# Attention and mixture of experts on one core: V in quadrants, a new order inside the turn, a cap on routing's steps

## Chip, core and metric

One core of a Trainium2 chip runs the whole program. The metric is the device time of one execution in microseconds. The kernel before takes 719.83 us in the median of three runs.

## What is computed

First a local and global attention (4 batches, 8 heads, 768 tokens, head size 64; a token sees itself, the 95 tokens before it and the first 8), then a mixture of 8 experts with two experts a token.

```python
scores = scale * np.matmul(q, k.transpose(0, 1, 3, 2)) + bias
scores = np.where(is_global | is_local, scores, -1e9)
a = np.exp(scores - np.max(scores, -1, keepdims=True))
x = np.matmul(a / (a.sum(-1, keepdims=True) + 1e-9), v)      # then (3072, 512)
noisy = x @ w_gate + np.log1p(np.exp(x @ w_noise)) * noise
top2 = ...                                                    # the two largest of 8, softmax over them
for e in range(8):
    out[mask] += top2_w * (np.maximum(x[mask] @ w1[e], 0.0) @ w2[e])
```

## The kernel before

The order of the work is written out by hand; nothing reorders it, and each engine takes its instructions in that order.

**The attention stage** is a loop of 48 turns, one for each unit: four heads of one block of 128 tokens (24 blocks, 6 a batch). A turn `n` handles several units at different depths: `score(n + 2)` (VectorE adds the bias and takes the maximum out of PSUM, ScalarE takes the exponential), `trans(n)` and `trans(n + 1)` (PE transposes the weights, ScalarE copies them), `gate_t` in every second turn (the tokens of a finished block are transposed on PE, copied by ScalarE, and copied in halves by GpSimd for a store), `product(n + 4)` (PE multiplies q and k), `attend(n - 2)` (PE multiplies the weights with V; each head has 65 columns, the last of ones, which gives the sum), `norm(n - 4)` (VectorE divides by that sum), and in every fourth turn `gate_l`, the products with the gate's weights, which read what ScalarE copied for `gate_t`.

The 128 tokens of a block are two halves of 64 (`s`), the four heads are two (`x`) by two (`y`). Each half sees a window of 168 keys: 96 before, 8 global, 64 own. `attend` sums the halves of a head in two rounds of matmuls; a matmul's place in the PE array is `tile_position`, and the first round of a block that has a block before it uses 64 rows of the array, the second up to 128:

```python
parts = [[(vs[g], 0, Q, 2), (vp[g], 0, NP + NG, 0)], [(vp[g], Q, NP + NG, 2), (vs[g], 0, P, 1)]]
```

`vs` holds the V rows of the block, `vp` the 96 rows before it and the 8 global ones. The sums of one unit lie in one PSUM bank; units alternate between banks 5 and 6. Scores lie in banks 0 and 1, transposed weights in 3 and 4.

**Routing** is a generator, `route(r)`, for each of 5 segments of blocks. It yields after each small VectorE instruction, and the loop takes one step of it at a `tick(place)` between the instructions of `score` (places 0 to 3) and `norm` (4 to 6), and up to 3 or 5 in `finish()` at the turn's end. A step that waits for another engine is marked, and is due again at a later place of the next turn. Segment `CLOSE` (number 2) closes expert 0's first 512 tokens: its masks are made on GpSimd (`mask`), summed on PE, and then expert 0's four tiles of tokens are gathered by GpSimd (`gather`, one a turn), copied (`whole_words`) and turned on PE (`turn`). After the loop what is left of that segment is run out, and the experts' products (`up`, `down`) begin.

In eight turns of the stage a split of w1 into a high and a low part runs as well (`split`: ScalarE and GpSimd).

## Time and profile before

| what | us or share |
|---|---|
| median of 3 runs (719.52 to 723.66) | 719.83 |
| the profiled execution's own time | 718.65 |
| its span | 716.9 |
| PE, VectorE, ScalarE, GpSimd busy | 97%, 64%, 61%, 45% |

An execution's time is its span and about 1.75 us around it. PE is TensorE's matmuls, PEld its weight loads, DVE is VectorE, ACT ScalarE, POOL GpSimd. A float32 matmul leaves two records. Times inside the trace count from the span's start. In the chain of waits a line is one piece of the path that ended last; a bracket in the timeline gives the idle time of the engine ahead of the instruction and who ended it.

### The profile page before, as it was taken

How to read it: one execution, taken by the hardware profiler on the slowest of the kernel's cores; microseconds unless marked ns; L12 is line 12 of the kernel's file. 1: busy time of each engine (PE TensorE's matmuls, PEld its weight loads, DVE VectorE, ACT ScalarE, POOL GpSimd, SP SyncE). 2: the span in 40 equal slices, each digit the busy share in tenths (PEclk: the TensorE clock that was granted, in tenths of full speed). 3: DMA queues.
4: the chain of work that ended last, by engine and by line, in shares of the span. 5: the costliest groups of instructions: out<-in, count | busy, mean ns of one | idle time of the engine just before them, and what ended most of it. 6: DMA issues, size and time to landing. Idle time of an engine off the chain costs nothing.

```text
span 716.9 us, 16231 instructions
## 1 busy us (share of the span) xinstructions
PE 692.7 (97%) x5769; PEld 618.3 (86%) x5769; DVE 457.1 (64%) x1473; ACT 440.0 (61%) x922; POOL 323.3 (45%) x416
## 2 busy tenths in 40 slices
PE   7999999999999799999999999999999999999995
PEld 5888888787789699999799989999899898889984
DVE  7669888977946376746564665576376756656600
ACT  6888787662437496546664685587467646755511
POOL 3363626481087362164606462644555344632222
PEclk9999999999999999999999999999999999999999
DMA  8996778685098784167916792587459547843233
GB/s 252 336 279 216 216 233 289 203 299 188 0 261 181 155 141 118 27 120 160 207 16 133 158 217 48 118 174 165 75 148 201 108 121 166 185 74 89 31 45 47
DMA packets 129913, 111.10 MB, mean 155 GB/s; under 512 B 51578, under 2 KB 96762, under 8 KB 129824
## 3 DMA queue, kind: packets, MB, share of 16 engines
q1 hardware_dynamic: 118416, 83.84, 42.9%
q0 software_dynamic: 11264, 25.89, 20.1%
q8 instruction: 47, 0.77, 0.5%
q14 instruction: 42, 0.34, 0.2%
q10 hardware_dynamic: 144, 0.26, 0.1%
HBM read 71.07 MB, written 27.59 MB: 138 GB/s over the span
## 4 chain that ended last, share of the span: by engine, by line
PE 64%; DVE 10%; issue 8%; DMA 7%; POOL 5%; ACT 5%; POOLq 0%; SPq 0%; ACTq 0%; DVEq 0%
PE bank L1397 20%; PE av L1144 19%; PE av L1167 7%; PE av L874 4%; PE sc L823 4%; PE at L853 3%; DMA xt<-xg 3%; DMA xg<-xd,ids 2%; DVE wall L196 2%; PE at L1107 1%; ACT hh L1088 1%; DVE w2l L196 1%; POOL out_dram L1120 1%; DVE ns L837 1%; DMA xd<-xt 1%
## 5 line engine op out<-in xcount | busy, mean ns | idle before, releaser
L1397 PE MATMUL bank<-xh,wall 128*128 128x384 f32 (+4 forms) x784 | 216.3, 343 | 1.1 <-ACT aside L1438 0.9
L1397 PEld LDWEIGHTS bank<-xh,wall 128*128 128x128 f32 x784 | 143.5, 188 | 6.7 <-DVE wall L196 1.4
L1397 PE MATMUL bank<-xl,wall 128*128 128x384 f32 (+4 forms) x392 | 133.4, 340 | 0.0
L1144 PE MATMUL av<-w2h,hh 128*128 128x512 f32 x304 | 120.3, 396 | 4.0 <-ACT aside L1176 2.3
L1120 POOL DMA_INDIRECT out_dram<-y,ids x40 | 63.8, 1596 | 127.7 <-ACT y L1117 124.4
L1144 PE MATMUL av<-w2h,hl 128*128 128x512 f32 x304 | 119.5, 393 | 0.3 <-DVE hl L1092 0.3
L1144 PE MATMUL av<-w2l,hh 128*128 128x512 f32 x304 | 119.1, 392 | 0.0
L196 DVE TENSOR_TENSOR wall<-raw,wall 128x512 fp32r<-128x512 f32 (+1 forms) x84 | 73.0, 875 | 48.4 <-ACT wall L195 48.3
L1092 DVE SCALAR_TENSOR_TENSOR hl<-bank,hh 128x384 fp32r<-128x384 f32 (+4 forms) x84 | 47.1, 561 | 66.5 <-ACT hh L1088 66.3
L195 ACT ACTIVATE wall<-raw 128x512 fp32r<-128x512 f32 (+1 forms) x84 | 58.0, 698 | 43.2 <-POOL raw L1252 43.2
L243 POOL DMA_INDIRECT xg<-xd,ids x53 | 58.8, 1109 | 52.1 <-DVE place L293 32.5
L840 ACT ACTIVATE a<-ns,mx 128x168 f32<-128x168 f32 (+1 forms) x192 | 67.9, 422 | 19.3 <-DVE mx L837 18.6
L1397 PEld LDWEIGHTS bank<-xl,wall 128*128 128x128 f32 x392 | 73.9, 188 | 2.7
L275 ACT ACTIVATE xg<-xt 128x1024 uint16<-128x1024 uint16 (+3 forms) x46 | 60.0, 1307 | 19.7 <-DMA xt<-xg 19.6
L1144 PEld LDWEIGHTS av<-w2h,hl 128*128 128x128 f32 x304 | 57.1, 188 | 14.1 <-DVE hl L1092 1.5
L1144 PEld LDWEIGHTS av<-w2h,hh 128*128 128x128 f32 x304 | 57.1, 188 | 14.0 <-ACT aside L1176 2.5
L1144 PEld LDWEIGHTS av<-w2l,hh 128*128 128x128 f32 x304 | 57.1, 188 | 9.3 <-DVE w2l L196 0.3
L837 DVE CUSTOM_DVE_ANT_0 ns<-sc,bias 128x168 f32<-128x168 f32 (+1 forms) x188 | 51.7, 319 | 18.4 <-PE sc L823 12.3
L1251 POOL TENSOR_TENSOR raw<-raw 128x256 f32<-128x256 f32 x28 | 21.9, 781 | 85.8 <-DVE wall L196 85.4
L874 PE MATMUL av<-vs,at 128*64 128x65 f32 (+1 forms) x768 | 57.3, 224 | 0.0
L235 POOL COPY xt<-y 128x256 uint16<-128x256 uint16 x96 | 35.2, 405 | 49.0 <-DVE y L890 46.9
L1088 ACT ACTIVATE hh<-bank 128x384 fp32r<-128x384 f32 (+4 forms) x84 | 41.8, 497 | 23.6 <-DVE bank L1467 16.0
(214 smaller groups left out, 1485.6 us busy)
## 6 DMA issues: line engine op xcount, KB each, us to landing
raw<-in_w SPq DMA_DIRECT2D x64, 256.0 KB
raw<-in_w SPq DMA_DIRECT2D x32, 512.0 KB
out_dram<-zero SPq DMA_DIRECT2D x14, 512.0 KB
vs<-in_v SPq DMA_DIRECT2D x24, 260.0 KB
xd<-xt SPq DMA_DIRECT2D x24, 256.0 KB
qbuf<-in_q SPq DMA_DIRECT2D x23, 256.0 KB
ks<-in_k SPq DMA_DIRECT2D x20, 272.0 KB
vp<-in_v SPq DMA_DIRECT2D x20, 195.0 KB
```

Of the source, the lines that this page charges most:

```text
L195: nc.scalar.activation(hi, src, AF.Copy)
L196: eng.tensor_sub(lo, src, hi.bitcast(F32))
L243: nc.gpsimd.indirect_dma_start(out=xg[e, t].bitcast(U16)[:m], out_offset=None, in_=xd[:n], in_offset=bass.IndirectOffsetOnAxis(ap=r, axis= ...
L275: nc.scalar.activation(words(x), xt.pop((e, t)).rearrange("p (h k) t -> p h (k t)", h=2), AF.Copy)
L837: nc.vector.tensor_tensor_reduce(out=ns[x][:, s, :w], in0=ps[:, s], in1=bias[:, u + x, s] if i else bias0[:, u + x, s], scale=-scale, scal ...
L840: nc.scalar.activation(A[n + x][:, s * w:(s + 1) * w], ns[x][:, s, :w], AF.Exp, bias=mx[x][:, s:s + 1], scale=-1.0)
L874: nc.tensor.matmul(ps[s * Q:(s + 1) * Q, h], a[r:z, part * P + q0:part * P + q0 + Q], t[r:z, c], start=k == 0 and (n == 1 or h == 0), stop ...
L1088: nc.scalar.activation(inner(e)[0][j][:, f, :src.shape[1]], src, AF.Relu)
L1120: ins = nc.gpsimd.indirect_dma_start(out=out, out_offset=bass.IndirectOffsetOnAxis(ap=r, axis=0), in_=y, in_offset=None, bounds_check=N + ...
L1144: nc.tensor.matmul(ps, x[j][:, f, cols], w[:, f], start=n == 0, stop=n == 3 * FC - 1)
L1167: nc.tensor.matmul(to, w[:, f, cols], x[:, f], start=n == 0, stop=n == 3 * FC - 1)
L1397: nc.tensor.matmul(ps, wb[c % 2][u][:, 2 * a + k], x[v][:, 2 * b + k], start=start and n == 0, stop=stop and n == 5, skip_group_check=True)
```

## The change

`attend` gives every head's two halves as eight matmuls of up to 128 rows and then eight of 64 x 64, which are placed in the four quadrants of the array. For that the second head of a pair (`x` = 1) has its halves and its V rows in another order: the exponentials are written to other columns, which are shifted by 24, the host lays V out anew in two tiles of 128 rows for each block (`vp` now has 128 rows, one transfer, instead of 96 and 8 in two), and the two heads of a pair sum into two banks. All units use both banks, in three places by turns. `norm` comes first in the turn, `attend` comes ahead of `product`, and the ticks have new places. Each of the first three segments may take 7, 8 or 9 steps a turn.

```diff
+        if b in AV and "av" in pools:
+            return pools["av"][:, AV.index(b)]
...
-                nc.sync.dma_start(vp[g][:NP], v[b, i - 1, P - NP:])
-                if i <= 4:
-                    nc.sync.dma_start(vp[g][NP:], v[b, 0, :NG])
+                nc.sync.dma_start(vp[g], v[b, i, 1])
...
+        PACE = {0: 7, 1: 8, 2: 9}
+        left = {}
...
         def begin():
+            left.update(PACE)
             for x, _ in active:
                 x.ready = {WAIT: 4, WAIT + 1: 6}.get(x.ready, 0)
...
             for y in sorted(active, key=lambda y: y[1] != CLOSE):
-                if y[0].ready <= place:
+                if y[0].ready <= place and left.get(y[1], 1) > 0:
                     return go(y)
...
-                    nc.scalar.activation(A[n + x][:, s * w:(s + 1) * w], ns[x][:, s, :w], AF.Exp,
+                    a = (1 - s) * w + Q - GQ if x and i else s * w
+                    nc.scalar.activation(A[n + x][:, a:a + w], ns[x][:, s, :w], AF.Exp,
                                          bias=mx[x][:, s:s + 1], scale=-1.0)
-                    tick(2 * x + s)
+                    tick(3 + 2 * x + s)
...
-            ps = pav[g, u // 2] = bank("av")[:, :4 * D1].rearrange("p (h d) -> p h d", h=4)
+            c0 = n // 2 % 3 * 2 * D1
+            ps = pav[g, u // 2] = av[:, :, c0:c0 + 2 * D1].rearrange("p x (y d) -> p x y d", y=2)
+            rounds = [[(s, x, vs, s, 0, P) for x in range(2) for s in range(2)]]
             if i:
+                rounds = [
+                    [(0, 0, vp, 0, 0, NP + NG), (1, 0, vs, 1, 0, P), (0, 1, vs, 1, 0, P), (1, 1, vs, 2, 0, P)],
+                    [(0, 0, vs, 2, 0, Q), (0, 1, vp, 0, Q, Q), (1, 0, vp, 2, Q, GQ), (1, 1, vp, 0, 0, Q)],
+                ]
+            for k, parts in enumerate(rounds):
+                for y in range(2):
+                    for s, x, t, part, r, m in parts:
+                        c = ((x * 2 + u // 2) * 2 + y) * D1
+                        nc.tensor.matmul(ps[s * Q:(s + 1) * Q, x, y], at[x][r:r + m, part * P + y * Q:][:, :Q],
+                                         t[g][r:r + m, c:c + D1], start=k == 0 and y == 0,
+                                         stop=k + 1 == len(rounds),
                                          tile_position=(r, s * Q), skip_group_check=True)
...
                 begin()
+                if n >= 4:
+                    norm(n - 4)
                 if n + 2 < NPAIR:
                     score(n + 2)
                 trans(n)
...
+                if n >= 2:
+                    attend(n - 2)
                 if n + 4 < NPAIR:
                     product(n + 4)
                 if n == NPAIR - 2:
-                    attend(n - 2)
-                if n >= 4:
-                    norm(n - 4)
-                if n == NPAIR - 2:
                     gate_t(NT - 2)
-                elif n >= 2:
-                    attend(n - 2)
```

On PE, turn 26 of the loop (a unit without a block before it) stands before as follows; `at` are the transposed weights, `m` is the bank of tokens and gate, `sc` the scores, `av` the products with V:

```order
L853 MATMUL at<-ident,a_185 128x128 x3
L853 MATMUL at<-ident,a_186 128x128 x3
L371 MATMUL m<-ident,y_98 128x128 x4
L823 MATMUL sc<-ks,qbuf_113 64x168 x8
L874 MATMUL av<-vs,at 64x65 x8
L393 MATMUL m<-pair,wgn 32x128 x8
```

The same turn after:

```order
L872 MATMUL at<-ident,a_188 128x128 x3
L872 MATMUL at<-ident,a_189 128x128 x3
L378 MATMUL m<-ident,y_98 128x128 x4
L894 MATMUL av<-vs,at 64x65 x8
L837 MATMUL sc<-ks,qbuf_117 64x168 x8
L400 MATMUL m<-pair,wgn 32x128 x8
```

V and the scores have changed places; what reads the tokens' copy (`m<-pair`) is still the last of the turn.

On GpSimd, at the end of the stage, before: `wall` are the closing segment's masks, `xt<-y` a block's copies of tokens, `xg<-xd` the gathers of expert 0, `xg<-xg` the copies of what was gathered.

```order
L555 TENSOR_SCALAR wall<-iota_p,aside 128x128 x10
L235 COPY xt<-y_98 128x2x128 x4
L243 DMA xg<-xd,ids_87 128x1024
L235 COPY xt<-y_97 128x2x128 x4
L243 DMA xg<-xd,ids_87 128x1024 x2
L235 COPY xt<-y_98 128x2x128 x4
L243 DMA xg<-xd,ids_87 128x1024
L235 COPY xg<-xg 128x2x128 x4
L235 COPY xt<-y_97 128x2x128 x4
L235 COPY xg<-xg 128x2x128 x12
```

The same place after:

```order
L562 TENSOR_SCALAR wall<-iota_p,aside 128x128 x10
L242 COPY xt<-y_98 128x2x128 x4
L242 COPY xt<-y_97 128x2x128 x4
L250 DMA xg<-xd,ids_87 128x1024 x3
L242 COPY xt<-y_98 128x2x128 x4
L242 COPY xt<-y_97 128x2x128 x4
L250 DMA xg<-xd,ids_87 128x1024
L242 COPY xg<-xg 128x2x128 x16
```

The gathers stand a turn later, and the fourth stands behind the last copies of tokens, with all sixteen copies behind it.

## Rows read from the trace of the kernel before

**Rows 1.** The page: span, and busy time of each engine

```profile
span 716.9 us, 16231 instructions
PE 692.7 (97%) x5769; PEld 618.3 (86%) x5769; DVE 457.1 (64%) x1473; ACT 440.0 (61%) x922; POOL 323.3 (45%) x416
```

**Rows 2.** Busy time by stretch: length, engines, granted clock, DMA share, GB/s

```profile
30.20:41.95 11.75, 11.75 (x249) 10.35 (x245) 7.02 (x46) 10.37 (x30) 5.20 (x7) 1.00 1.06 335
53.74:71.08 17.34, 16.75 (x333) 14.44 (x329) 15.80 (x109) 14.25 (x40) 6.35 (x15) 1.00 0.71 223
137.51:146.35 8.84, 8.04 (x126) 6.62 (x122) 7.43 (x44) 5.41 (x15) 8.53 (x15) 1.00 0.11 36
```

**Rows 3.** Chain of waits, 69 to 77 us: start, length, engine, tile, line

```profile
69.34 0.73 PE sc L823 x16
...
71.15 0.81 PE at L853 x6
...
72.69 1.08 PE av L874 x32
...
74.58 0.44 PE m L371 x4
...
76.69 0.57 PE m L393 x16
```

**Rows 4.** Timeline of PE's matmuls, 69.7 to 70.5 us

```profile
69.75 0.32 PE L823 MATMUL sc<-ks,qbuf 64*64 64x168 f32 x4
...
70.24 0.22 PE L874 MATMUL av<-vs,at 64*64 64x65 f32 x1
...
70.26 0.22 PE L874 MATMUL av<-vp,at 40*64 40x65 f32 x1
...
70.30 0.22 PE L874 MATMUL av<-vs,at 64*64 64x65 f32 x1
...
70.47 0.27 PE L874 MATMUL av<-vs,at 128*64 128x65 f32 x1
```

**Rows 5.** Timeline of VectorE, 70 to 72.3 us

```profile
70.23 0.33 DVE L837 CUSTOM_DVE_ANT_0 ns<-sc,bias 128x168 f32<-128x168 f32 x1 [1.10 <-PE sc L823]
...
71.25 0.16 DVE L885 TENSOR_SCALAR den<-av 128x4 f32<-128x4 f32 x1
...
72.06 0.20 DVE L536 TENSOR_TENSOR aside<-lg,carry 128x48 f32<-128x48 f32 x1
```

**Rows 6.** Timeline of ScalarE: a split at 32 us, the turn at 70 us

```profile
32.38 0.64 ACT L195 ACTIVATE xh<-raw 128x512 fp32r<-128x512 f32 x1
32.90 1.41 ACT L840 ACTIVATE a<-ns,mx 128x168 f32<-128x168 f32 x4
...
70.61 1.41 ACT L840 ACTIVATE a<-ns,mx 128x168 f32<-128x168 f32 x4 [0.30 <-DVE mx L837]
71.92 0.84 ACT L855 ACTIVATE at<-at 128x384 f32<-128x384 f32 x2
...
74.67 0.85 ACT L855 ACTIVATE at<-at 128x384 f32<-128x384 f32 x2
75.42 0.59 ACT L380 ACTIVATE pair<-m 128x512 f32<-128x512 f32 x1
```

**Rows 7.** Timeline of GpSimd, 136 to 163 us: masks, fourth gather, copies

```profile
136.96 6.59 POOL L555 TENSOR_SCALAR wall<-iota_p,aside 128x128 fp32r<-128x128 f32 x10 [7.25 <-DVE aside L563]
...
152.83 1.03 POOL L243 DMA_INDIRECT xg<-xd,ids  x1
...
156.64 0.75 POOL L235 COPY xt<-y 128x256 uint16<-128x256 uint16 x2 [0.44 <-DVE y L890]
157.33 4.74 POOL L235 COPY xg<-xg 128x256 uint16<-128x256 uint16 x12
```

**Rows 8.** All gathers (line 243), issue to landing; chain, expert 0's first product

```profile
DMA to landing us min/median/max: 3.3/5.0/8.3
...
163.21 1.66 PE at L1107 x6
```

More of the change, by code (lines that the diff above doesn't have):

```diff
@@ L660, in load_v @@
             vs[g] = aw.tile([P, HD], F32, name="vs", bufs=4)
[L661 removed]
+            nc.sync.dma_start(vs[g], v[b, i, 0])
             if i:
                 vp[g] = vpb[g % 4]
[L664 to L666 removed]
+                nc.sync.dma_start(vp[g], v[b, i, 1])
         if windowed:
[L669 removed]
+            vpb = [ac.tile([P, HD], F32, name=f"vp{j}") for j in range(4)]
             pairs.append(ac.tile([P, 2 * Dm], F32, name="pair"))
@@ L722, in tile_local_global_attention_then_moe @@
             biases(bias0, dist0, range(H))
-            abuf = [ac.tile([P, 2 * WIN], F32, name=f"a{j}") for j in range(4)]
+            abuf = [ac.tile([P, 2 * WIN + j % 2 * (Q - GQ)], F32, name=f"a{j}") for j in range(4)]
+            for j in 1, 3:
+                nc.gpsimd.memset(abuf[j][:, :Q - GQ], 0.0)
         else:
@@ L797, in finish @@
                 n = 5 if y[1] >= CLOSE else 3
-                while n and y in active and y[0].ready <= END:
+                while n and y in active and y[0].ready <= END and left.get(y[1], 1) > 0:
                     go(y)
@@ L851, in trans @@
             x = A.pop(n)
-            for k, c in enumerate((0, 2 * WIN - P, NP + NG) if i else (0, P)):
+            if n % 2 and i:
+                parts = [Q - GQ + NP + NG, Q - GQ + WIN + GQ, 0]
+            else:
+                parts = [0, 2 * WIN - P, NP + NG] if i else [0, P]
+            for k, c in enumerate(parts):
                 nc.tensor.transpose(ps[:, k * P:(k + 1) * P], x[:, c:c + P], ident)
@@ L861, in attend @@
             g, u, b, i = geo(n)
-            ps = pav[g, u // 2] = bank("av")[:, :4 * D1].rearrange("p (h d) -> p h d", h=4)
             at = [AT.pop(n + x) for x in range(2)]
-            heads = [(at[x], 2 * y + x, y * Q) for x in range(2) for y in range(2)]
-            parts = [[(vs[g], 0, P, 0)], [(vs[g], 0, P, 1)]]
+            c0 = n // 2 % 3 * 2 * D1
+            ps = pav[g, u // 2] = av[:, :, c0:c0 + 2 * D1].rearrange("p x (y d) -> p x y d", y=2)
+            rounds = [[(s, x, vs, s, 0, P) for x in range(2) for s in range(2)]]
             if i:
-                parts = [[(vs[g], 0, Q, 2), (vp[g], 0, NP + NG, 0)], [(vp[g], Q, NP + NG, 2), (vs[g], 0, P, 1)]]
-            n = len(parts[0])
-            for k in range(n):
-                for a, h, q0 in heads:
-                    c = slice((u // 2 * 4 + h) * D1, (u // 2 * 4 + h + 1) * D1)
-                    for s in range(2):
-                        t, r, z, part = parts[s][k]
-                        nc.tensor.matmul(ps[s * Q:(s + 1) * Q, h], a[r:z, part * P + q0:part * P + q0 + Q], t[r:z, c],
-                                         start=k == 0 and (n == 1 or h == 0), stop=k + 1 == n,
+                rounds = [
[9 more added lines that the diff above has]
+                                         stop=k + 1 == len(rounds),
                                          tile_position=(r, s * Q), skip_group_check=True)
@@ L1060, in tile_local_global_attention_then_moe @@
     rings.update(sc=[0, 1], m=[2])
+    del pools["av"]
     with ExitStack() as mctx:
+        pm = mctx.enter_context(tc.tile_pool(name="pm", bufs=1, space=bass.MemoryType.PSUM))
+        pools.update({b: pm for b in AV})
         mc = mctx.enter_context(tc.tile_pool(name="mc", bufs=1))
@@ L1498, in tile_local_global_attention_then_moe @@
         wov = lc.tile([P, NT, E], F32, name="wov")
-        for (a, z), (ixf, sl, we) in zip(SEG, kept):
+        for (a, z), (ixf, sl, we) in zip(SEG, (kept[r] for r in range(len(SEG)))):
             w = z - a
@@ L1570 @@
     vx[..., :D] = v.transpose(0, 2, 1, 3).reshape(B, NB, P, H, D)
+    if 1 <= int(inputs["n_local"]) <= NP + 1 and 0 <= int(inputs["n_global"]) <= NG:
+        v0 = vx.reshape(B, NB, P, H // 4, 2, 2, D + 1).transpose(5, 0, 1, 2, 3, 4, 6).reshape(2, B, NB, P, -1)
+        half = P // 2
+        vx = np.zeros((B, NB, 2, P, 2, v0.shape[-1]), v.dtype)
+        vx[:, :, 0, :, 0] = v0[0]
+        vx[:, 0, 0, :, 1] = v0[1][:, 0]
+        vx[:, 1:, 0, half:, 1] = v0[1][:, 1:, :half]
+        vx[:, 1:, 1, :half, 1] = v0[1][:, 1:, half:]
+        first = [np.broadcast_to(x[:, :1, :NG], (B, NB - 1, NG, x.shape[-1])) for x in v0]
+        before = [np.concatenate([x[:, :-1, P - NP:], y], axis=2) for x, y in zip(v0, first)]
+        vx[:, 1:, 1, :NP + NG, 0] = before[0]
+        vx[:, 1:, 1, half:, 1] = before[1][:, :, :half]
+        vx[:, 1:, 0, 2 * half - NP - NG:half, 1] = before[1][:, :, half:]
+        vx = vx.reshape(B, NB, 2, P, -1)
+    else:
+        vx = vx.reshape(B, NB, P, -1)
     arrays = {
```

33 lines of the change are left out of this document (19 added, 14 removed).

## The prediction

> **What bounds the kernel now.** I read the page first: 716.9 us, PE busy 97% of it, VectorE 64%, ScalarE 61% [rows 1]. The change touches the attention stage, the first 160 us, 48 turns of the loop (a turn is one unit of four heads). So I read that stage by the table of stretches [rows 2], one turn by the chain of waits [rows 3], PE's single matmuls [rows 4], what VectorE and ScalarE do meanwhile [rows 5, 6], and the end of the stage on GpSimd's timeline and the chain [rows 7, 8].
>
> A turn on PE is a row of blocks end to end [rows 3]: transposes of the weights 0.81, in every second turn transposes of tokens 0.44, products of the next scores 0.73, V 1.08, in every fourth turn the gate's products 0.57. So a short turn takes 0.81 + 0.73 + 1.08 = 2.62, one with tokens 3.06, one with the gate too 3.63. In the four turns 30.20 to 41.95 PE is busy without a gap (11.75 of 11.75) while ScalarE has 10.37. With routing, 53.74 to 71.08, VectorE has 15.80 of 17.34 and PE waits 0.6 [rows 2]. PE is the bound, but two engines stand close behind.
>
> **Part 1, V in quadrants.** A V matmul of 65 columns leaves two records. Two of them run side by side, and the next pair starts 59 ns later (70.24, 70.30) [rows 4]. A unit has 16 matmuls in 8 pairs: 8 x 2 x 0.059 = 0.94, and 1.08 with two drains. After, the first round has 8 matmuls in 4 pairs, the second has 8 in 2 groups of four: 6 x 2 x 0.059 = 0.71. That spares 0.235 a unit. Four at once is seen on the score products: four records of 0.30 each fit into 0.32 (69.75) [rows 4], so they start within 0.02. Forty units have a block before them (6 blocks a batch, the first has none: 5 x 2 x 4); the other eight keep their 8 matmuls. 40 x 0.235 = **-9.4**. Lower bound: the second of a pair starts 20 ns after the first (70.24, 70.26); were that the spacing of four, a group would take 0.08 and the gain would be 40 x (0.235 - 4 x 0.021) = 6.0. I take 9.4, since the row with four at once is the nearer one.
>
> The drains count too: after 70.30 the next different form starts at 70.47, 0.17 instead of 0.06 [rows 4]. Before, a turn changes form three times (transposes to scores, inside V, V to transposes). After, three too (transposes to V, inside V, scores to transposes): nothing.
>
> **Part 2, V ahead of the scores.** PE's blocks only change places, but now the score products end the turn. The chain behind them is long: product end 69.34 + 0.73 = 70.07, VectorE starts at 70.23, ScalarE's first exponential at 70.61, its copies of the transposed weights at 71.92 [rows 3, 5, 6]. The copy of the tokens starts 0.75 after the first of those copies (74.67, 75.42) and lasts 0.59 [rows 6]. Before, V's 1.08 lay between the product and the next turn; after, nothing does. And norm stands ahead of the scores on VectorE: it needs V's end + 0.16, takes 71.25 to 72.06 = 0.81 [rows 5], and V ends 0.73 before the product does, so it ends 0.24 after the product. With the product's end as 0: scores 0.24, exponentials 0.24 + 0.38 = 0.62, copies + 1.31 = 1.93, token copy + 0.75 = 2.68, done 3.27.
> - Turn with the gate: PE comes to the gate's products at 0.81 + 0.44 + 0.845 + 0.73 = 2.83, but they need the token copy: 3.27 + 0.04. A new wait of 0.48. Queued behind it are the next transposes, and on ScalarE the gate's own copy with the next exponentials. Before, the copy ended at 75.42 + 0.59 = 76.01 and PE came at 76.69: 0.7 to spare [rows 3, 6]. Ten such turns: **+4.8**.
> - Short turn: the first copy ends at 1.93 + 0.48 = 2.41, PE wants its bank again at 2.39; with a signal's 0.04 some 0.05 of wait, a dozen times: **+0.6**.
> - The product waits for the scores' readers: 0.24 + 1.1 = 1.34 against 1.66 when PE gets there. Fits.
>
> The price of this part is bounded by 0 (VectorE and ScalarE run ahead enough) and by about 9 (with routing's instructions in between, below).
>
> [...] All units now share two banks, so each V block has to wait until norm of the unit before has read. Unhidden, 0.81 x 48 would be 39 us. By the rows norm's last read ends 0.24 + 0.08 after the product, and V starts at 0.81 or 1.25, so it costs nothing.
>
> **Part 3, the splits of w1.** Eight turns from 30.2 to 53.7 also carry a split on ScalarE, 0.52 from start to start (32.38, 32.90) [rows 6]. It is issued behind the token copy, so the next exponentials start late: walking four turns as above gives 3.97 + 2.56 + 2.83 + 2.77 = 12.13, against 11.75 measured. These eight turns lose 0.8 where parts 1 and 2 counted a gain of about 0.8 (8 x 0.235 less 2 x 0.48 and 2 x 0.05): **+1.5**.
>
> **Part 4, the cap and the new places of routing's steps.** No instruction is added; VectorE's sum stays. From 53.74 to 71.08 PE's part falls from 16.75 to about 15.4, and VectorE's 15.80 becomes the larger: at most 1.5 of 17.34 can go. The cap spares PE's 0.6 of waiting there and in the later segments perhaps 2 in all. Against that, steps inside a score delay the exponentials, and in the gate's turns everything in part 2. I take **0**, from -2 to +4.
>
> **Part 5, the closing segment's masks.** GpSimd makes ten in 6.59 from 136.96 on [rows 7], and PE waits for the last of them: turns 42 and 43 (137.51 to 146.35) take 8.84 [rows 2], where their blocks (3.06 + 2.62) and ten sums over the masks (168 columns each, 0.15 by the 0.059 of 65 columns) make 7.2. After, those sums stand one turn later, while the masks start at about the same place of turn 42, so PE has another short turn of its own work before it waits: most of the 1.6 goes, **-1.4** (0 to -1.6).
>
> **Part 6, the end of the stage.** Expert 0's tokens are gathered, copied on GpSimd, turned on PE. Before, the fourth gather is issued at 152.83, ahead of the last token copies; these end at 157.33, twelve copies of 4.74 follow, and the first product of expert 0 starts at 163.21 [rows 7, 8]. After, the fourth gather stands behind the last token copies, and sixteen copies behind it. Counted from the same last token copies: these to 157.33 or so, gather 1.03, then 16 x 0.395 = 6.3 end near 164.8 instead of 162.07. If the gather itself is late (5.0 in the median, 8.3 at most [rows 8]) the last four copies wait for it until 157.5 + 8.3 = 165.8, + 1.6. So PE starts later by 2.7 to 5.3; nothing else is ready for it. I take **+3.0**, since the sixteen copies bound it and the queues are emptier by then.
>
> **Part 7, V's loads.** vp grows from 96 rows to 128: 20 x 65 KB more, sixteen small transfers less. They are asked for three blocks ahead, and no wait in the stage names them: 0. Uncovered, 1.3 MB at the 335 GB/s of the table [rows 2] is 3.9.
>
> **Sum.** -9.4 + 4.8 + 0.6 + 1.5 + 0 - 1.4 + 3.0 = -0.9. The profiled execution took 718.65 (span 716.9 and 1.75 around it), the median is 719.83: forecast 718.9.
>
> **Rivals.**
> 1. V's gain arrives (0.25). VectorE and ScalarE run far enough ahead that the gate does not wait, and the even routing saves its 2: -9.4 + 0.6 - 2 - 1.4 + 3.0 = -9.2, 710.6. For it: ScalarE has 12% of slack and a waiting turn lets VectorE catch up. Against: ScalarE works in order, and its chain starts a whole block of V later.
> 2. The gate's wait grows (0.18), on the other side. Seven of the ten gate turns carry routing steps inside the scores; four steps of 0.2 there delay the token copy by 0.8, and what is lost is not made up. Then 7 x 0.8 = 5.6 more, with a late fourth gather (+2): 726.5. It decides over 1% from a gate wait of about 1.2 on.
> 3. The quadrants do not overlap in fours (0.05, part of the 0.18): the -9.4 is gone, 728.3.
> 4. The forecast, gain and waits cancelling: 0.57.
>
> About 1% (7.2 us) is what a measurement of this kernel can tell from no change. Faster by over 1% 0.25, within 0.57, slower 0.18. The likeliest case alone spans 713 to 725; the range takes rival 1's time and most of rival 2's: 710 to 728.
>
> **What would show it.** Part 1: V's block 0.85 instead of 1.08, four records starting within 0.03. Part 2: waits of PE's gate product for ScalarE's token copy, ten of about 0.5, and gate turns of 3.9; if absent, rival 1. Part 3: four turns from about 30 on of 12.1. Part 5: turns 42 and 43 together 7.4. Part 6: the first product of expert 0 some 9.6 us after the last copies of tokens set out on GpSimd (163.21 - 156.64 = 6.6 before). The forecast is wrong if V's block stays near 1.08, or if the gate does not wait.

## The result and the profile after

The changed kernel takes 730.14 us (median of four, 729.14 to 730.74), the kernel before 719.67 beside it: a ratio of 1.014, with an interval of 1.009 to 1.019. It is slower by over 1%, and outside the range of 710 to 728, on the side of rival 2.

The page of the changed kernel, span and busy time, answering to [rows 1]:

```profile
span 729.0 us, 16221 instructions
PE 694.0 (95%) x5769; PEld 608.6 (83%) x5769; DVE 458.5 (63%) x1473; ACT 441.5 (61%) x922; POOL 322.6 (44%) x418
```

No engine is busier than before by more than 1.5: PE 694.0 for 692.7, VectorE 458.5 for 457.1. So the twelve us are waiting, and more than twelve: V's blocks got shorter (below), and PE's busy time should have fallen. Work that runs out ahead of a wait counts as busy in this table (in turn 10 below PE's gap is 0.51 in the matmuls and 0.75 in the weight loads), and work at a lower clock counts for longer (turn 46's six transposes of weights take 1.54 from 164.01 on, at a granted clock of 0.50; turn 21's take 0.85 at 1.00). The table of stretches of the changed kernel: the three that answer to [rows 2], then turns 0 to 46 of the attention loop, then turns 38 to 43:

```profile
31.33:43.30 11.97, 11.45 (x248) 9.21 (x244) 6.80 (x45) 10.71 (x30) 5.20 (x7) 1.00 0.88 294
55.13:72.56 17.43, 15.99 (x329) 12.74 (x330) 15.34 (x104) 14.14 (x38) 6.32 (x15) 1.00 0.76 237
144.51:153.62 9.11, 7.57 (x126) 5.84 (x123) 7.61 (x43) 5.26 (x13) 7.72 (x14) 1.00 0.02 5
...
7.47:167.43 159.96, 144.95 (x2746) 114.03 (x2747) 118.80 (x754) 119.75 (x333) 69.38 (x142) 0.98 0.78 251
...
126.83:153.62 26.79, 21.71 (x378) 16.50 (x378) 21.77 (x143) 16.14 (x42) 10.15 (x20) 1.00 0.57 186
```

The same two last stretches of the kernel before:

```profile
6.93:155.22 148.29, 145.53 (x2747) 123.90 (x2747) 118.95 (x754) 117.87 (x333) 72.14 (x145) 1.00 0.82 256
...
124.04:146.35 22.31, 21.19 (x372) 17.64 (x370) 20.04 (x136) 15.15 (x42) 10.58 (x19) 1.00 0.59 196
```

PE is idle for 148.29 - 145.53 = 2.8 in these 47 turns before, and for 159.96 - 144.95 = 15.0 after. What it waits for, by the table of waits of the changed kernel, 7.4 to 170.4 us (engine, tile, line, who was waited for: total, times, longest; PE is the gap in the matmuls, PEld the gap in the weight loads):

```profile
PE m L400 <- ACT pair L387: 5.0, 8, 1.0
PE av L894 <- DVE y L911: 3.5, 7, 1.0
PE lg L413 <- ACT aside L403: 2.5, 1, 2.5
PE sc L837 <- DVE den L906: 1.0, 1, 1.0
...
PEld m L400 <- ACT pair L387: 7.9, 10, 1.3
PEld av L894 <- DVE y L911: 6.1, 11, 1.2
...
PEld sc L837 <- PE av L894: 3.0, 6, 0.7
```

Three things stand there: the gate's products for ScalarE's token copy (line 387), V for norm's multiply on VectorE (line 911) with the next products queued behind V, and one long pause (line 403). By stretch, from the starts of the turns in both timelines (a turn starts with the first transpose of line 872, before 853):

| stretch | before | after | difference |
|---|---|---|---|
| start of turn 0 | 6.93 | 7.47 | +0.54 |
| turns 0 to 5 | 16.26 | 15.67 | -0.59 |
| turns 6, 7 | 7.01 | 8.19 | +1.18 |
| turns 8 to 15 (splits) | 23.54 | 23.80 | +0.26 |
| turns 16 to 37 (routing) | 70.30 | 71.70 | +1.40 |
| turns 38 to 43 (closing segment) | 22.31 | 26.79 | +4.48 |
| turns 44 to 46 | 8.87 | 13.81 | +4.94 |
| turn 47 to expert 0's first product | 7.99 | 10.41 | +2.42 |
| the experts, to the span's end | 553.65 | 551.12 | -2.53 |

The sum is +12.1, the difference of the two spans.

### The profile page after: what moved, and what is told of

Same layout as the page of the kernel before. It is cut to its first block, busy times and chain, and to the rows that moved or that the text cites. A ratio compares the mean times of both kernels' runs of the same rounds, so it can differ in the third digit from the quotient of the medians.

```text
span 729.0 us, 16221 instructions
## 1 busy us (share of the span) xinstructions
PE 694.0 (95%) x5769; PEld 608.6 (83%) x5769; DVE 458.5 (63%) x1473; ACT 441.5 (61%) x922; POOL 322.6 (44%) x418
## 4 chain that ended last, share of the span: by engine, by line
PE 64%; DVE 11%; issue 8%; ACT 8%; POOL 5%; DMA 3%; another core or an unknown queue 1%; SPq 0%; POOLq 0%; ACTq 0%; DVEq 0%
PE bank L1418 23%; PE av L1165 20%; PE av L1188 7%; PE av L894 3%; PE at L872 3%; PE sc L837 2%; DMA xt<-xg 2%; DVE ns L851 2%; ACT a L855 1%; ACT at L874 1%; PE at L1128 1%; POOL out_dram L1141 1%; DVE wall L203 1%; DVE w2l L203 1%; PE sc L1128 1%
## 5 line engine op out<-in xcount | busy, mean ns | idle before, releaser
L855 ACT ACTIVATE a<-ns,mx 128x168 f32<-128x168 f32 (+1 forms) x192 | 69.6, 421 | 30.9 <-DVE mx L851 29.5
L837 PE MATMUL sc<-ks,qbuf 64*64 64x168 f32 (+1 forms) x752 | 44.4, 315 | 8.3 <-DMA ks<-in_k 5.4
```

What stands on the lines that cost most here:

```text
L837: nc.tensor.matmul(SC[n + x][y * Q:(y + 1) * Q, s], qs[b, j][r, 2 * i0 + s, u + y], ks[b, j][r, u + y, k0:k0 + w], start=True, stop=True, ...
L855: nc.scalar.activation(A[n + x][:, a:a + w], ns[x][:, s, :w], AF.Exp, bias=mx[x][:, s:s + 1], scale=-1.0)
```

## The experiments

18 runs (after_again is the changed kernel a second time), each beside the kernel before on its chip. "38 to 43" is the length of these turns, "expert 0" its first product, both in the profiled execution; the ratio has its 95% interval.

| kernel | median us | ratio to before | 38 to 43 | expert 0 |
|---|---|---|---|---|
| before | 719.67 | 1 | 22.3 | 163.2 |
| changed | 730.14 | 1.014 (1.009 to 1.019) | 26.8 | 177.8 |
| after_again | 732.16 | 1.017 (1.010 to 1.025) | 26.8 | 176.5 |
| quad_old_order | 722.61 | 1.006 (1.002 to 1.011) | 22.0 | 168.6 |
| order_alone | 736.28 | 1.027 (1.021 to 1.033) | 25.2 | 183.3 |
| v_ahead_alone | 729.26 | 1.013 (1.010 to 1.016) | 22.9 | 173.3 |
| v_last | 776.66 | 1.084 (1.080 to 1.088) | 36.3 | 219.8 |
| gate_first | 727.43 | 1.013 (1.008 to 1.017) | 25.9 | 167.9 |
| norm_whole | 736.17 | 1.024 (1.013 to 1.034) | 28.2 | 178.5 |
| no_cap | 727.65 | 1.012 (1.003 to 1.021) | 24.8 | 173.0 |
| close_open | 730.66 | 1.015 (1.009 to 1.022) | 30.8 | 176.9 |
| score_whole | 731.08 | 1.016 (1.008 to 1.024) | 23.0 | 174.6 |
| gather_early | 725.40 | 1.010 (1.006 to 1.014) | 26.8 | 170.8 |
| zero_early | 728.55 | 1.012 (1.007 to 1.017) | 26.8 | 172.1 |
| gate_gather_norm | 730.72 | 1.015 (1.007 to 1.022) | 27.4 | 174.7 |
| gate_gather | 725.30 | 1.006 (1.003 to 1.010) | 25.8 | 168.5 |
| gate_gather_score | 727.26 | 1.010 (1.008 to 1.012) | 23.1 | 167.0 |
| gate_gather_zero | 724.95 | 1.006 (1.002 to 1.010) | 25.9 | 169.9 |
| quad_old_steps_last | 732.83 | 1.016 (1.012 to 1.020) | 24.9 | 174.7 |
| before_zero | 719.04 | 0.996 (0.993 to 1.000) | 22.3 | 165.0 |

The expert stage, which none of these edits touches, takes 551 to 559 in these profiled executions. So a single edit is read from its own stretch first, and from the total only where its interval allows it.

**The change taken apart: quadrants or order.** quad_old_order is the changed kernel with the loop body of before:

```diff
-                if n >= 4:
-                    norm(n - 4)
                 if n + 2 < NPAIR:
                     score(n + 2)
...
-                if n >= 2:
-                    attend(n - 2)
                 if n + 4 < NPAIR:
                     product(n + 4)
+                if n >= 4:
+                    norm(n - 4)
+                if n >= 2:
+                    attend(n - 2)
...
-        PACE = {0: 7, 1: 8, 2: 9}
+        PACE = {}
```

(and the ticks at their old places). order_alone is the reverse, the kernel before with norm first, `attend` ahead of `product` and the new ticks; v_ahead_alone has only `attend` ahead of `product`; v_last is the changed kernel with only `attend` put back behind `product`.

> The quadrants alone: the changed kernel with the order of before (scores, then the products of the next scores, then norm, then V; routing's steps at their old places and without the cap). Theory A, the order is what costs, not the quadrants: V's blocks last 0.85 here too and nothing else moves, so the 9.4 of part 1 arrives and the time is about 710. Theory B, the two shared banks cost: each V block must wait until norm has read the unit before, and norm now stands behind four score instructions of VectorE; a wait of 0.8 or more in each of 48 turns, so 719.7 - 9.4 + 48 x 0.8 = about 749, above the changed kernel's 730.1.

> The order alone: the kernel before, with norm ahead of the scores, V ahead of the next scores' products and routing's steps at the new places; V keeps its 16 matmuls in pairs and its two alternating banks, no cap. Theory A, the order is what costs: the whole loss stays and the quadrants' gain is missing, 730.1 + 9.4 = about 739. Theory B, the loss comes mostly from V waiting for norm through the shared banks (6.1 + 3.0 in the profile of the changed kernel) and from the one stall of 3.7 in turn 45: neither is here, so 719.7 + 8 (gate's waits) = about 728 or less. The prediction's own terms give 719.7 + 4.8 + 0.6 + 1.5 - 1.4 + 3.0 = 728.2.

> The kernel before with one move: V ahead of the products of the next scores. Norm stays behind the scores, routing's places stay, V keeps its pairs and its two alternating banks. This splits the order alone (736.3 against 717.3, 19 lost) into V's move and the rest. The prediction charged V's move with 4.8 + 0.6 and 1.5: 724 to 727; an extra change of form between V's last pair and the score products adds 0.14 a turn, 6: up to 732. If norm ahead of the scores and routing's steps inside them are what costs, this one is near 722 and the gate's waits are under 0.3 each; if V's place costs, it is 730 or more with gate's waits of 0.8.

> The changed kernel with one move undone: V again behind the products of the next scores, norm still ahead of the scores. Theory B: V comes to PE 0.73 later in the turn, so most of its waits for norm (6.1, and 3.0 behind them) are covered by the score products, and the score products no longer stand at the turn's end, which spares the gate's wait (8.6): about 730.1 - 9 - 6 = 715. Theory A by order of norm (norm ahead of the scores holds VectorE up, wherever V stands): within 2 of 730.1. A rival: the products of the next scores then wait for VectorE's score reads, which norm has pushed back by 0.81: 40 x 0.2 to 0.4 of new waits, 725 to 735.

Turns 0 to 46 in the table of stretches of order_alone, v_ahead_alone, quad_old_order and v_last, one fence each:

```profile
6.91:174.34 167.43, 154.87 (x2747) 123.44 (x2747) 123.79 (x755) 119.78 (x332) 69.75 (x143) 0.98 0.72 228
```

```profile
7.30:164.20 156.90, 150.64 (x2746) 120.79 (x2746) 118.41 (x748) 117.67 (x332) 72.00 (x145) 1.00 0.78 241
```

```profile
7.14:159.10 151.96, 144.21 (x2747) 112.80 (x2747) 122.04 (x753) 118.01 (x333) 72.66 (x147) 1.00 0.82 259
```

```profile
6.98:209.07 202.09, 166.37 (x2746) 124.36 (x2747) 120.52 (x755) 121.69 (x332) 68.55 (x142) 0.96 0.63 200
```

The order alone costs 736.3 - 717.3 = 19 (the kernel before took 717.3 on that chip). V's move alone costs 729.3 - 719.6 = 9.6. The gate waits there as in the changed kernel, by the table of waits of v_ahead_alone:

```profile
PEld m L393 <- ACT pair L380: 7.9, 10, 1.4
```

And a short turn takes 2.76 instead of 2.62: V's pairs and the score products are now neighbours, and one more change of form (the shape in which a matmul uses the array) comes in; PE's busy time in turns 0 to 46 rises by 150.64 - 145.53 = 5.1. The quadrants spare that one, since their last eight matmuls are 64 x 64 as the score products are: in turn 21 of the changed kernel the products start 0.05 behind the last group of V's records (74.19, 74.24). The rest, another 9, comes with norm ahead of the scores and the steps' new places; about half of it stands in two turns of order_alone's profile. Turns 25 and 26 take 11.1 there, 6.3 in v_ahead_alone: five instructions of routing stand ahead of norm and the scores on VectorE, PE waits 1.8 for a score read, and the granted clock falls to 0.76 in turn 25. Turn 25 in the table of stretches:

```profile
88.98:95.23 6.25, 4.47 (x46) 3.39 (x43) 4.71 (x25) 2.73 (x9) 1.75 (x5) 0.76 0.93 294
```

In the new order the quadrants, with the cap, take 9.9 off PE's busy time (154.87 to 144.95). With no_cap (below), which is order_alone with the quadrants, all four corners are on record, as ratios to the kernel before: quadrants alone 1.006, order alone 1.027, both 1.012 (1.003 to 1.021, two executions). So the quadrants gain some 1.5% in the new order, where they also spare a change of form, and lose 0.6% in the old one. The order costs 2.7% with V in pairs; with the quadrants it costs 0.5%, which the intervals do not tell from nothing.

Why do the quadrants gain nothing in the old order? First, the form. PE in turn 21 of quad_old_order, where V does not wait for norm (its multiply ends at 73.71 on VectorE, V starts at 74.11):

```profile
72.58 0.87 PE L872 MATMUL at<-ident,a 128*128 128x128 f32 x6
73.38 0.80 PE L837 MATMUL sc<-ks,qbuf 64*64 64x168 f32 x16
74.11 0.27 PE L894 MATMUL av<-vp,at 104*64 104x65 f32 x1
...
75.12 0.44 PE L872 MATMUL at<-ident,a 128*128 128x128 f32 x2
```

The turn takes 2.54, where the kernel before had 2.62 and the changed kernel has 2.38. V's first eight matmuls have up to 128 rows and stand behind the score products of 64, so here the quadrants add a change of form, and 0.08 of the 0.24 is left: about 3 in forty turns, as an estimate. V ahead of the products is thus not only norm's affair: it also puts V's last matmuls next to products of the same form. Second, V waits for norm, by the table of waits of quad_old_order:

```profile
PEld av L894 <- DVE y L911: 10.9, 21, 1.8
```

A gap of 0.24 stands ahead of V in turn 21 too, without a wait, so about 10.9 - 21 x 0.24 = 6 of it is waiting.

Both expectations missed (710 and 749): V waits for norm in 21 turns, not in 48 and not in none. The two banks are shared, and norm stands behind the scores there, so the change puts norm first; and then V must go ahead of the products. That is v_last: norm delays VectorE's score reads by 0.8, the products wait for these, V behind them, and norm of the next turn for V. VectorE's waits in v_last:

```profile
DVE den L906 <- PE av L894: 64.8, 38, 3.8
```

It takes 776.7 where 715 and 725 to 735 had been expected: with norm ahead of the scores, V has to go ahead of the products. The reverse, V ahead and norm behind, was run with alternating banks alone (v_ahead_alone). The quadrants without either move took 722.6. The traces show the price of the shared banks: these waits stand between V and norm although the units use different columns. In the changed kernel none of norm's readings of V's sums (lines 906 and 911) runs beside a V block, and ten V blocks start 0.05 to 0.06 behind norm's multiply of the unit before; in the kernel before, whose banks alternate, 19 of the 48 multiplies run beside a V block, for up to 0.42. order_alone, whose banks alternate too, has no wait of V for norm's multiply in its table of waits. What would come of leaving the waits out, no run here shows.

**The gate's wait.** gate_first moves the token transposes to the head of the turn, so that ScalarE copies the tokens ahead of the exponentials:

```diff
+                if g >= 0 and not odd:
+                    gate_t(g)
                 if n + 2 < NPAIR:
                     score(n + 2)
...
-                    else:
-                        gate_t(g)
```

> The changed kernel with the gate's token transposes (and so ScalarE's copy of the tokens) at the head of the turn, ahead of the scores. If the gate's waits (8.6 in 11 turns) are what costs, they go and the time is about 730.1 - 8 = 722. Rival: the copy of 0.59 now stands ahead of ScalarE's exponentials, so ScalarE's chain ends 0.5 later and the copies of the transposed weights hold up the next turn instead: 729 to 731, with the wait moved to the transposes.

Turns 0 to 46 in the table of stretches of gate_first:

```profile
6.89:156.13 149.24, 140.77 (x2747) 111.67 (x2747) 118.70 (x755) 119.37 (x333) 68.98 (x142) 1.00 0.80 257
```

The wait is gone from the table of waits, and the 47 turns take 149.2 instead of 160.0. Half of these 10.7 is the pause of turn 45, which does not come here: gather_early (below), the same kernel up to turn 46 and without a pause too, takes 161.23 - 6.88 = 154.4 for these turns, so the gate's move is worth 5.1. The median keeps 2.7 of it all, which the intervals do not tell from nothing: from turn 47 to expert 0 it takes 11.8 instead of 10.4, and the experts 557.7 instead of 551.1. So the mechanism is shown in its stretch, and the sum of the whole is not.

**V's wait for norm and the closing turns.** Four kernels with one edit each on the changed one. norm_whole moves the three ticks of `norm` behind its multiply; no_cap has `PACE = {}`, close_open `PACE = {0: 7, 1: 8}`; score_whole runs the four score instructions in one piece:

```diff
-                    tick(3 + 2 * x + s)
+        for x in range(4):
+            tick(3 + x)
```

> The changed kernel with one edit: norm's three instructions run in one piece, and the three steps of routing that may stand between them come behind the multiply. Theory N, routing's steps inside norm are what makes V wait for norm (6.1 in 11 turns, all of them turns with routing, and 3.0 behind them on the next products): these waits fall to 2 or less in the closing segment's turns 38 to 42 and elsewhere, the end of the attention stage comes 4 to 6 earlier, the time 724 to 726. Rival: VectorE has more to do in these turns than PE, wherever the steps stand (5.57 busy in turn 40), so the waits change their place only: 728 to 732.

> The changed kernel without the cap on routing's steps in a turn. If the cap does what part 4 took for possible (it spares PE's waits of up to 2, by putting steps into emptier turns), the time rises by 2 to 5, most of it in turns 16 to 19 and 28 to 31, to 732 to 735. Rival: the cap only pushes the same steps into later turns and so delays the closing segment: without it turns 38 to 43 (26.8 in the changed kernel, 22.3 before) get shorter by 2 or more, and the time falls to 727.

> The changed kernel with the cap kept for the first two segments and taken off the closing one. Without any cap turns 38 to 43 took 24.8 instead of 26.8, and turns 16 to 35 took 3.2 more. If the two are independent, this kernel keeps the gain of the one and loses nothing at the other: 2 less than the changed kernel, about 724 without a pause. Rival: the closing segment's later steps then come at the same time as the next segment's, and turns 42 to 46 give the 2 back: 726.

> The changed kernel with one edit: the four score instructions of VectorE run in one piece, and the four places for routing's steps come behind them. Theory T, routing's steps inside the scores hold up ScalarE's exponentials and so the gate's token copy and V (rival 2 of the prediction): in turns with routing the gate's waits (0.6 to 1.2) shrink to about 0.5, turns 38 to 40 (15.1) get shorter by 2, and the time falls by 3 to 5, to 722 to 724 if no pause comes in. Rival, VectorE is simply the longer engine in these turns, and the steps are only moved behind: no change, 726 to 730. The four turns without routing from turn 8 on (11.97) stay in both.

Theory N fell: norm in one piece makes the closing turns longer, 28.2. Without the cap turns 38 to 43 take 24.8, 2 less, and turns 16 to 35, 55.13 to 120.39 in the changed kernel, take 3.2 more. The two did not come apart as hoped: close_open has turns 38 to 41 at 18.5 instead of 17.7, and in turn 42 V waits 2.0 for norm (the turn takes 8.9, at a granted clock of 0.76). score_whole has the effect. Its turns 38 to 43:

```profile
128.28:151.28 23.00, 20.11 (x377) 15.96 (x373) 21.31 (x134) 14.70 (x43) 11.60 (x25) 1.00 0.75 248
```

23.0 instead of 26.8, near the 22.3 of before, with VectorE busy 21.3 of it. How VectorE loses its time in the changed kernel shows its timeline of turn 39 (line 472 and 590 are steps of routing, 906 to 911 norm, 851 the scores), and PE's beside it:

```profile
131.20 0.67 DVE L472 SCALAR_TENSOR_TENSOR aside<-aside 128x40 f32<-128x40 f32 x3
...
132.29 0.42 DVE L911 TENSOR_TENSOR y<-av,den 128x256 f32<-128x256 f32 x1
...
132.74 0.33 DVE L851 CUSTOM_DVE_ANT_0 ns<-sc,bias 128x168 f32<-128x168 f32 x1
...
133.88 0.32 DVE L851 CUSTOM_DVE_ANT_0 ns<-sc,bias 128x168 f32<-128x168 f32 x1
```

```profile
132.77 0.27 PE L894 MATMUL av<-vp,at 104*64 104x65 f32 x1 [0.95 <-DVE y L911]
...
134.36 0.79 PE L837 MATMUL sc<-ks,qbuf 64*64 64x168 f32 x14 [0.24 <-DVE aside L480]
```

V waits 0.95 for the multiply, and the products, 1.6 later, wait again for the last score read: PE runs in VectorE's steps. But score_whole gives it back elsewhere: the gate's turns 22, 26, 34 and 36 take 20.5 instead of 14.7, as the steps collect there and the gate waits up to 1.4. That v_ahead_alone has 22.9 in turns 38 to 43, order_alone, without shared banks, 25.2, and no_cap 24.8 says the same: 0.6 comes with V's place, 2.3 with norm's and the steps' place on VectorE, 2.0 with the cap, and the quadrants with their shared banks give 0.4 back.

**The end of the stage.** gather_early lets one step through in the last turn, which is the fourth gather:

```diff
                 if n == NPAIR - 2:
+                    tick(6)
                     gate_t(NT - 2)
```

> The changed kernel with one edit: in the last turn of the loop one step of routing is let through ahead of GpSimd's last token copies, so that the fourth gather stands ahead of them as before. By part 6 of the prediction expert 0's first product comes 6.6 to 7 after these copies set out instead of 9.3, and the time falls by 2.5 to 3, to 727. Rival: the transfer or the sixteen copies behind it set the end anyway (6.3 for the copies), and nothing changes: 730.

GpSimd's timeline in the changed kernel, answering to [rows 7], and the first product of expert 0 in its chain, as in [rows 8]:

```profile
168.53 0.75 POOL L242 COPY xt<-y 128x256 uint16<-128x256 uint16 x2 [3.79 <-DVE y L911]
169.43 1.03 POOL L250 DMA_INDIRECT xg<-xd,ids  x1
170.47 6.31 POOL L242 COPY xg<-xg 128x256 uint16<-128x256 uint16 x16
...
177.84 1.20 PE at L1128 x4
```

and GpSimd's in gather_early:

```profile
160.03 1.03 POOL L250 DMA_INDIRECT xg<-xd,ids  x1 [0.16 <-PE m L378]
...
162.77 0.74 POOL L242 COPY xt<-y 128x256 uint16<-128x256 uint16 x2 [0.96 <-DVE y L911]
163.45 6.25 POOL L242 COPY xg<-xg 128x256 uint16<-128x256 uint16 x16
```

From the last token copies to expert 0 it takes 9.3 in the changed kernel, 8.0 here (170.78 - 162.77), 6.6 before. So the late gather is 1.3 of it; the other 1.4 are four copies more, which stay. The median falls by 4.7, to 725.4, though the intervals overlap. In the profiles most of the gain is turn 45, which has no pause here (2.54).

**The pause.** In the changed kernel ScalarE waits 3.7 us in turn 45, though the gate's products that it needs stand at 156.66 to 157.3 in PE's timeline, and the view names nothing of this core that it waited for ("remote": another core or an unknown queue). after_again is the same kernel a second time; zero_early asks for the clearing of the output earlier, and before_zero is the kernel before with the same line:

```diff
-                at(63 + 4 * j, zero_out, j)
+                at(47 + 4 * j, zero_out, j)
```

> The changed kernel itself, a second time. In its first profile turn 45 takes 6.78, with a wait of 3.7 of ScalarE that no instruction explains; a kernel that is the same up to turn 46 (the fourth gather early) takes 2.54 there. Theory S1, the pause comes by chance in single executions: turn 45 takes 2.5 to 2.8 here, the span is some 725, and the loss of the change is 4 smaller than the first profile shows. Theory S2, the pause belongs to this program's code and transfers: turn 45 takes 6.5 or more again, 729 to 731.

> The changed kernel with the eight transfers that clear the output asked for 8 turns earlier (turns 23 to 37 instead of 31 to 45), and nothing else. The pause in turn 45 (6.78 and 6.36 in two profiles; ScalarE waits 3.6 for nothing that an instruction explains) falls into a stretch in which these transfers and 2 MB of raw w2 keep the DMA engines busy all the time. Theory D, it is the full DMA queues that hold something of PE up: without the clearing transfers there the pause is gone or under 1, turn 45 takes 2.5 to 3.5, the time falls by 3 to 4 to 727. Rival, something in the program at this place: 6.4 or more again, 730 to 732.

> The kernel before with the clearing transfers 8 turns earlier and nothing else: the measure for what this edit does where there is no pause in turn 45 (2.76). No change, within 2 of the kernel before, if the transfers only mattered through the pause; 2 to 3 faster if the kernel before loses something of the kind too; slower by 1 to 3 if the transfers now meet loads that the turns 23 to 30 wait for.

ScalarE in the timeline, and three stretches, of the changed kernel; then the first two of these stretches in zero_early:

```profile
160.29 0.28 ACT L403 ACTIVATE aside<-m 128x128 f32<-128x128 f32 x1 [3.68 <-remote]
...
155.00:160.00 5.00, 3.04 (x70) 2.23 (x68) 2.40 (x14) 1.61 (x5) 3.87 (x5) 0.97 0.99 273
160.00:165.00 5.00, 4.38 (x55) 3.67 (x56) 1.94 (x11) 2.83 (x10) 1.90 (x6) 0.50 1.05 408
165.00:170.00 5.00, 4.78 (x81) 3.89 (x79) 2.50 (x16) 3.26 (x9) 1.32 (x3) 0.84 0.65 249
```

```profile
155.00:160.00 5.00, 4.94 (x98) 4.01 (x95) 3.63 (x22) 3.52 (x12) 4.39 (x7) 1.00 0.97 325
160.00:165.00 5.00, 4.35 (x96) 3.37 (x94) 2.66 (x16) 3.70 (x10) 3.00 (x7) 1.00 0.99 386
```

The pause came again at the same place in after_again (turn 45 at 6.36), as S2 has it, and not in zero_early (2.54), as D has it. But the DMA engines are as full in zero_early, and gather_early, whose program is the same up to turn 46, has no pause. In gate_gather_zero it is there in spite of the earlier clearing (turns 45 and 46 at 4.98 and 4.22). And before_zero, which should not have one, has one in its profiled execution: turn 44 takes 5.20 instead of 3.63, and that execution took 725.89 where the median is 719.04. So such pauses come in either order, here in stretches with DMA at 0.9 or more (0.92 in that turn 44, 1.04 in turn 45 of the changed kernel, 1.05 and 0.90 in the two turns of gate_gather_zero), and the changed kernel had one in both of its profiles. What holds PE there stays open.

**Do the losses add up?** The combinations, made of the edits above (norm: as norm_whole; score: as score_whole; zero: as zero_early), and the quadrants in the old order with all steps of routing behind norm:

> Three edits on the changed kernel together: the gate's token transposes at the head of the turn, norm in one piece, the fourth gather ahead of the last token copies. With the gate's waits gone (attention stage 9.9 shorter in the profile of the first of these alone, of which the total kept 2.7), the end of the stage 2.5 shorter, and V's waits for norm down by 4: expert 0 starts near 161, and the time is 717 to 720, level with the kernel before or 1 to 2 under it, if the expert stage takes its 553 to 555. Rival: what is won ahead of the experts is given back behind (the expert stage took 551.1 in the changed kernel and 557.7 with the gate first): 724 or more.

> Two edits on the changed kernel: the gate's token transposes at the head of the turn and the fourth gather ahead of GpSimd's last token copies. The gate's waits (7.8) are gone, as in the kernel with the first edit alone, and the end of the stage is shorter by 2.2 (11.8 from turn 47 to expert 0 there, 9.55 with the early gather). Expert 0 then starts near 165.5, 2.3 behind the kernel before, and the time is 719 to 721. Rival: the expert stage takes more, since its transfers are not ready any earlier: 723 to 726.

> Three edits on the changed kernel: the gate's token transposes at the head of the turn, the fourth gather early, the four score instructions in one piece with routing's steps behind them. The steps behind the scores made turns 38 to 43 3.8 shorter (23.0 instead of 26.8) and lost 4 in the gate's turns 22, 26, 34 and 36, where PE waits 1.3 to 1.4 for the token copy; with the gate first that wait is gone. So turns 38 to 43 take 22 to 23, expert 0 starts 3 to 4 earlier than with the two edits alone (168.5), and the time is 718 to 721, level with the kernel before. Rival: pauses of 2 or more in the stretch of full DMA queues (turns 42 to 46) take it back: 724.

> The changed kernel with three edits, one for each loss that a single edit has shown so far: the gate's token transposes at the head of the turn, the fourth gather early, the clearing transfers 8 turns earlier. With the first two turns 45 and 46 took 9.2 (5.2 in a kernel without a pause) and expert 0 started at 168.5. If the pause goes with the transfers, expert 0 starts near 164.5 and the time is 718 to 721, within 1% of the kernel before; what is then left of the loss are the closing turns 38 to 43 (25.7 against 22.3). Rival: the pauses only change their place, 724 or more.

> The quadrants with the order of before, no cap, and routing's steps all behind norm's last instruction. With the old places V waits 10.9 in 21 turns for norm, which stands behind the scores and the steps inside them. Theory T: the waits in turns with routing go, those of about 0.4 in short turns stay (5 or so), and the time is 717 to 719 against 722.6 with the old places. Rival: VectorE is the longer engine in these turns and its steps come too late for the closing segment: 722 or more.

gate_gather is 0.6% slower than the kernel before, against 1.4% for the change: gate and gather together take about half of the loss away. Its turns 8 to 35 take 84.8, 2.9 less than before (30.68 to 115.51, and 30.20 to 117.95), so there the quadrants do pay; turns 38 to 43 lose 3.5 and the rest goes at the end of the stage, pauses among it. None of the further edits adds to it: zero 0.6%, score 1.0% (its closing turns are short, 23.1, but turn 47 to expert 0 takes 11.8), norm 1.5%. quad_old_steps_last missed by 14: V's waits for norm fall from 10.9 to 4.4 in 18, which is the gap of 0.24 that stands there without a wait, and a short turn still takes 2.54, so it is the form that holds it there; but turns with routing get longer (18 and 30 take 5.06 each instead of 4.39 and 4.40), the closing ones too, 24.9 instead of 22.0. No kernel beats the one before beyond its interval, except before_zero by 0.4%, which has nothing of the change.

## Why the prediction was wrong, by its own steps

- **Part 1, V in quadrants: right.** PE in the changed kernel's timeline, turn 21:

```profile
73.34 0.27 PE L894 MATMUL av<-vp,at 104*64 104x65 f32 x1
...
74.07 0.22 PE L894 MATMUL av<-vs,at 64*64 64x65 f32 x1
74.07 0.23 PE L894 MATMUL av<-vp,at 64*64 64x65 f32 x3
...
74.24 0.34 PE L837 MATMUL sc<-ks,qbuf 64*64 64x168 f32 x4
```

Four records start within 0.01, and the block takes 74.24 - 73.34 = 0.90 (0.85 forecast). Turn 21 takes 2.38 where 0.81 + 0.845 + 0.73 = 2.385 was forecast and 2.62 stood before. Rival 3 is out. The count of form changes was right as well, and it holds for this order only: in the old one the same blocks leave 0.08 (quad_old_order).
- **Part 2, the gate's wait: its mechanism right to the tenth, its price too small.** In turn 10 the chain came as walked: ScalarE's copies of the weights 2.05 after the products' end (1.93), the token copy done at 3.38 (3.27), PE there at 2.93 (2.83), its start 0.05 behind the copy's end (0.04):

```profile
38.82 0.85 ACT L874 ACTIVATE at<-at 128x384 f32<-128x384 f32 x2
39.56 0.59 ACT L387 ACTIVATE pair<-m 128x512 f32<-128x512 f32 x1
```

```profile
38.96 0.74 PE L837 MATMUL sc<-ks,qbuf 64*64 64x128 f32 x16
40.20 0.64 PE L400 MATMUL m<-pair,wgn 128*32 128x128 f32 x16 [0.51 <-ACT pair L387]
```

PE's gap is 0.51 (0.48), and 5.4 in all with the lone block's 0.4 (4.8). But the turn takes 4.01 where 3.50 less 0.235 was due, so 0.75 was lost, the gap in the weight loads. The two gaps differ by 0.24 here, and by 0.24 to 0.31 in the nine of these waits that show in both; that the block ahead of the wait runs out in that time and the next one starts anew is the author's reading. In eleven turns the gaps in the weight loads are 8.6 instead of 4.8.
- **Part 2, V behind norm, "so it costs nothing": wrong, and with part 4 the main failure.** That V waits for norm of the unit before held: 46 of the 47 blocks that have one before them start 0.05 or more behind its multiply, and the last stands ahead of it in the program. The price was worked out for a turn without routing, and in such turns it mostly holds (0.9 in turn 6). In turns with routing VectorE comes late to norm and the scores. V waits 6.1 in 11 turns, 4.2 of it in turns 17 to 42, and the products behind it 3.0. The banks are only one way by which that reaches PE: order_alone, where V does not wait for norm, loses 2.9 in turns 38 to 43 as well; there the score products wait for VectorE's reads, up to 1.0. Rival 2 had the steps in the scores delay the gate; they delayed norm and the score reads, for which V and the products now wait.
- **Part 3, the splits: right.** 11.97 for four turns, 12.13 forecast, 11.75 before.
- **Part 4, routing's steps: wrong.** It had 0, from -2 to +4; turns 16 to 41 alone lose 1.4 + 4.2 where the parts together had forecast a gain. That VectorE's sum stays was right, and it was the wrong question: what matters is where the steps stand beside norm and the scores. The cap did what was said of it in turns 16 to 35, 3.2, and cost 2 in turns 38 to 43, which the prediction had not seen.
- **Part 5, the closing masks: wrong.** Turns 42 and 43 take 9.1, not 7.4. No wait for the masks is left in them, as forecast, but PE waits in turn 42 for norm (0.6) and for VectorE's reads of the scores (1.3).
- **Part 6, the end of the stage: right.** 9.3 (9.6 forecast, 6.6 before); the late gather is half of it, the four copies the other half.
- **Part 7:** no wait for V's loads stands in the table of waits.
- **Not in the sum:** turn 6, +1.25 (V waits 0.9 for norm, the gate 1.3), and the pause in turn 45, +4.0, with turn 46 at a granted clock of 0.50 behind it, +0.95.

The spans lie 13 further apart than the sum had it (+12.1 against -0.9), and the experts gave 2.5 back, which is within what they vary by. These 15 or so are what the gate's waits took beyond the forecast (8.6 - 4.8 = 4), VectorE's chain through norm (6.1 for V, of which 0.17 a turn stands in turns without a wait too, and up to 3.0 for the products behind it) and the pause with the slow clock behind it (5). The three overlap in part, and no run here splits them to the tenth.

## What to carry to other kernels

When a change lets all units share a buffer, walk the reader's engine in its fullest turn, not in the emptiest one: here norm was free in a plain turn and cost most where VectorE also carried routing (4.2 of V's 6.1 us of waits in turns 17 to 42). Price a new wait on PE by the gap in the weight loads of a similar wait (0.75 in turn 10, which lost 0.75), less the gap that stands there without a wait (0.24 ahead of V in quad_old_order), and not by the idle time of the matmuls (0.51). And take a move apart from what makes it necessary, in both directions: quadrants, norm first and V ahead came as one, and only the four corners show that the quadrants gain in the new order alone, that the order costs far more with V in pairs (2.7%) than with quadrants (0.5%), and that no corner beats the kernel before.

## What the runs showed of the hardware

A change of matmul form cost time here even without a wait: one more in a turn made the short turn 2.76 instead of 2.62 (V's pairs ahead of the score products) and 2.54 instead of 2.38 (V's blocks of 128 rows behind them). PE also stopped in the middle of a block with nothing to wait for that the profile shows. In gate_gather_norm a V matmul stands alone behind a gap of 2.08 that no semaphore explains, while DMA is at 1.08, and the clock's mean falls to 0.93:

```profile
34.25 0.21 PE L894 MATMUL av<-vp,at 64*64 64x65 f32 x1 [2.08 <-issue]
...
30.00:35.00 5.00, 2.90 (x50) 2.35 (x53) 1.44 (x12) 3.16 (x8) 1.20 (x1) 0.93 1.08 341
```

In the changed kernel PE was idle for 2.5 us ahead of 160.6, and the granted clock was 0.50 from 160 to 165 and 0.84 in the next five us. In gate_gather's turns 45 and 46, with PE busy 3.79 of 5.15 and 2.06 of 4.02 us, it stayed at 1.00.
